# Decoding float64 weights in three instructions instead of four: the sign bit through ScalarE's leaky unit

## The chip, the core and the metric

The kernel runs on one core of a Trainium2 chip. A core has five engines that run at the same time, each with its own queue of instructions in a fixed order: TensorE (PE, matrix products, with PEld for its weight loads), VectorE (DVE), ScalarE (ACT), GpSimd (POOL) and SyncE (SP, which here only issues DMAs). An engine waits on semaphores for what another has to deliver, and whatever stands behind a waiting instruction on the same queue waits too. The metric is the device time of one execution in microseconds, less is better.

## What is computed

The reference chains three blocks. Arrays are numpy's.

```python
# attention over clusters: B, H, S, D = 2, 8, 768, 64
mask = q_assign[:, :, :, None] == k_assign[:, :, None, :]
scores = np.where(mask, scale * q @ k.T, -1e9)
attn = softmax(scores)
x = (attn @ v) reordered to (1536, 512)
# first block: w1, w2 (512, 1024), w3 (1024, 1024), w_out (1024, 512)
x = ((x @ w1) * (x @ w2)) @ w3 @ w_out
# second block: w_in (512, 2048), w_out (2048, 512)
h = x @ w_in
out = (np.maximum(h, 0) + np.log1p(np.exp(-np.abs(h)))) @ w_out
```

The weight matrices come as float64. [...]

## The kernel before

**Stages.** Three stages follow one another. Attention (to about 375 us of the profiled execution) goes through 96 slots, six per head; in slot s PE computes the scores of slot s for the row minima (`mx_pe`, line 625), then those of slot s-9 again for the exponential (`st_pe`, 652), then the product with v of slot s-10 (`av_pe`, 668). The head pairs that come later are prepared in between: norms, transposes, the cluster assignment, and DMAs on SP's queue (`t_dma` 325, `m_dma` 443) that put the pieces of q and k in place. Beside all that the product w3 @ w_out is formed in 24 pieces of 128 x 512 (`w_step`, 579), so that the first block needs only `W3O` later. The first block (375 to 569 us) multiplies 512 tokens at a time by 8 chunks of w1 and w2 and by `W3O`; the second block (569 us to the end) by 16 chunks of w_in and w_out, with the softplus between the two on ACT, DVE and POOL (`sp1`, `sp2`, `sp3`, 1082 to 1107).

**The order of work.** Within attention the order on every engine is that of the code (`tc.manual_schedule`, line 911, up to the opening of the first block); from there on a planner orders the instructions by priority, its own costs and buffer limits, and `feed.take` is held behind the last evaluation (`tc.issue_after`).

**A decode.** A piece is a DMA of 512 KB into a raw tile of 128 x 1024 words (`load_w`, 74), low and high word of each number alternating. Four instructions of 128 x 512 follow:

1. ACT multiplies the high words, read as float32, by 2^-112 (line 63). This lowers the exponent so that, three bits further left, it is float32's.
2. DVE shifts the low words right by 29 (lines 104, 489, 764).
3. DVE takes the two top bits of the scaled high word, the sign among them, and puts them into the low word (108, 493, 768).
4. DVE shifts the high word left by three, which drops the sign bit, and ors the low word in (113, 498, 773).

Then ACT rounds to the PE's format (`act_copy(hi, d)`) and POOL subtracts for the remainder (`pool_sub`, line 66). 72 pieces are decoded: 24 in `w_step`, 5 through `Feed.part` in attention's last slots, and 43 through `decode` (16 + 16 + 11), 34 of them in the first block and 9 in the second.

**Where the steps stand in the slots.** `WT` (569) gives each of the 24 pieces its steps by slot: in the piece's slot 0 A (step 1, ACT) and b (step 2), in slot 1 c (step 3), in slot 2 d (step 4), after which the next raw piece is loaded (`w_load`, 504, a DMA on SP's queue, line 81, that waits until d has read the raw tile). A new piece begins every two and a half slots. From slot 76 (`WSLOT`, lines 1000 to 1008) five more pieces go through `feed.part`, one step per slot and four slots per piece; the first two are split and stored at once (`feed.take`, slots 79 and 83), which also puts the load of a next piece on SP's queue. That load waits until POOL has finished `wl`, the remainder, since POOL reads the raw tile. The softmax's denominators travel on the same queue: `av_ev` (687) writes a row out, `r_ev` (689) reads it back as r, lets DVE invert it (699, 702), and sends it round again (704, 708).

Of the kernel before, what the change touches and what calls it, by code (L numbers as in the profile page):

```python
# [8 lines left out]
F32 = mybir.dt.float32  # L9
F32R = mybir.dt.float32r  # L10
BF16 = mybir.dt.bfloat16
I32 = mybir.dt.int32
AF = mybir.ActivationFunctionType
ALU = mybir.AluOpType
# [13 lines left out]
def fused_kernel(ctx: ExitStack, tc, q, k, v, centroids, w1, w2, w3, wo, w_in, w_o2, out):  # L28
# [6 lines left out]
    nc = tc.nc  # L35
# [23 lines left out]
    def act_copy(o, i, scale=None):  # L59
        if scale is None:  # L60
            nc.scalar.activation(o, i, AF.Copy)  # L61
        else:
            nc.scalar.activation(o, i, AF.Copy, scale=scale)

    def pool_sub(o, i, hi):
        nc.gpsimd.tensor_tensor(out=o, in0=i, in1=hi, op=ALU.subtract)  # L66

# [16 lines left out]
    def decode(pieces):  # L84

        wide, outs = [], []  # L90
        for t, o in pieces:
            if t.dtype == F32:
                if o is not None:
                    nc.vector.tensor_copy(o, t)
                outs.append(t if o is None else o)
            else:
                tv = t.rearrange("p (n t) -> p n t", t=2)
                lo, hi = tv[:, :, 0], tv[:, :, 1]
                hf = hi.bitcast(F32)
                act_copy(hf, hf, scale=2.0 ** -112)  # L100
                wide.append((lo, hi, hi if o is None else o.bitcast(I32)))
                outs.append(hf if o is None else o)
        for lo, _, _ in wide:
            nc.vector.tensor_scalar(
                out=lo, in0=lo, scalar1=29, scalar2=None, op0=ALU.logical_shift_right
            )
        for lo, hi, _ in wide:
            nc.vector.scalar_tensor_tensor(
                out=lo, in0=hi, scalar=-0x40000000, in1=lo,
                op0=ALU.bitwise_and, op1=ALU.bitwise_or,  # L110
            )
        for lo, hi, o in wide:
            nc.vector.scalar_tensor_tensor(
                out=o, in0=hi, scalar=3, in1=lo,
                op0=ALU.logical_shift_left, op1=ALU.bitwise_or,
            )
        return outs

    identF = cpool.tile([P, P], F32, name="identF")
# [351 lines left out]
    def w_scale(n):  # L471
        t = W3["r", n]
        if t.dtype != F32:
            hf = t.rearrange("p (n t) -> p n t", t=2)[:, :, 1].bitcast(F32)
            act_copy(hf, hf, scale=2.0 ** -112)

    def w_bits(n, step):

        t = W3["r", n]
        if step == 2:  # L480
            d = W3["d", n] = w3p.tile([P, 512], F32, tag="d", name=f"w3d{n}")
        if t.dtype == F32:
            if step == 2:
                nc.vector.tensor_copy(d, t)
        else:
            tv = t.rearrange("p (n t) -> p n t", t=2)
            lo, hi = tv[:, :, 0], tv[:, :, 1]
            if step == 0:
                nc.vector.tensor_scalar(
                    out=lo, in0=lo, scalar1=29, scalar2=None, op0=ALU.logical_shift_right  # L490
                )
            elif step == 1:
                nc.vector.scalar_tensor_tensor(
                    out=lo, in0=hi, scalar=-0x40000000, in1=lo,
                    op0=ALU.bitwise_and, op1=ALU.bitwise_or,
                )
            else:
                nc.vector.scalar_tensor_tensor(
                    out=d.bitcast(I32), in0=hi, scalar=3, in1=lo,
                    op0=ALU.logical_shift_left, op1=ALU.bitwise_or,  # L500
                )
        if step == 2:
            W3.pop(("r", n))
            w_load()

# [54 lines left out]
    def w3_end(n):  # L560
# [6 lines left out]


    WT = {
        "o": {0: "Ab", 1: "c", 2: "d", 6: "s"},  # L570
        "3": {0: "Ab", 1: "c", 2: "d", 3: "T", 4: "hl", 7: "m", 8: "p", 9: "q", 10: "e"},
    }
    WF = {
        "A": w_scale, "b": lambda n: w_bits(n, 0), "c": lambda n: w_bits(n, 1),
        "d": lambda n: w_bits(n, 2), "s": wo_split, "T": w3_turn, "h": w3_hi, "l": w3_lo,
        "m": w3_acc, "p": w3_add, "q": w3_out, "e": w3_end,
    }

# [160 lines left out]
    class Feed:  # L739
# [13 lines left out]
        def part(self, i, step):  # L753

            e = self.fly[i]
            t = e[0]
            if t.dtype == F32:
                return
            tv = t.rearrange("p (n t) -> p n t", t=2)
            lo, hi = tv[:, :, 0], tv[:, :, 1]  # L760
            if step == 0:
                act_copy(hi.bitcast(F32), hi.bitcast(F32), scale=2.0 ** -112)
            elif step == 1:
                nc.vector.tensor_scalar(
                    out=lo, in0=lo, scalar1=29, scalar2=None, op0=ALU.logical_shift_right
                )
            elif step == 2:
                nc.vector.scalar_tensor_tensor(
                    out=lo, in0=hi, scalar=-0x40000000, in1=lo,
                    op0=ALU.bitwise_and, op1=ALU.bitwise_or,  # L770
                )
            else:
                nc.vector.scalar_tensor_tensor(
                    out=hi, in0=hi, scalar=3, in1=lo,
                    op0=ALU.logical_shift_left, op1=ALU.bitwise_or,
                )
                self.fly[i] = (hi.bitcast(F32), e[1])

        def take(self, n=1):
# [123 lines left out]
    }  # L903


    WALL = "AbcdsThlmpqe"
    WSLOT = 76
    W0 = 4
    wk = [W0]

    with tc.manual_schedule():
        act_dma = nc.scalar.dma_start
        load_qk(0, [0])
        centroid_load()
        load_qk(0, [1], act_dma)
        nc.scalar.preload_act_table_set("natural_log_exp_and_others")
        w_load()
        w_load()
        t1_pe(0, 0)
        t1_pe(0, 1)  # L920
        centroid_prep()
        t1_ev(0, 0)
        t1_ev(0, 1)
        t1_pe(0, 2)
        t1_pe(0, 3)
        t1_ev(0, 2)
        t1_ev(0, 3)
        centroid_turn()
        norm_sq(0, 0)
        norm_sq(0, 1)  # L930
        load_qk(1)
        t_first()
        sims_pe(0, 0)
        sims_pe(0, 1)
        sims_ev(0, 0)
        sims_ev(0, 1)
        norm_sum(0, 0)
        norm_sum(0, 1)
        simsT_pe(0)
        norm_root(0)  # L940
        for n in range(W0):
            w_step(n, WALL[:1])
        norm_rec(0, 0)
        norm_rec(0, 1)
        norm_rec(0, 2)
        t_dma(0, 1)
        t_dma(0, 0)
        assign(0, 0)
        assign(0, 1)
        back_pe(0)  # L950
        back_ev(0)
        m_dma(0, 1, act_dma)
        w_load()
        load_v(0)
        for n in range(W0):
            w_step(n, WALL[1:])
        for s in range(NSLOT + ML + AL):
            j = s - ML
            a = j - AL
            if s < NSLOT:  # L960
                mx_pe(s)
                mx_red(s)
            if s and s % QC == 0 and s <= NSLOT:
                m_row(s // QC - 1)
            weights = s >= ML
            if weights:
                w_step(wk[0], "hlpqe")
            if a > 0 and a % 3 == 0:
                av_ev(a // 3 - 1)
            for tab in (PE1, EV1):  # L970
                for f, *x in tab.get(s, ()):
                    f(1, *x)
            if s == 4:
                load_qk(2)
            if s == 8:
                load_v(1)
            steps(PE, s)
            steps(EV, s)
            if 0 <= j < NSLOT:
                st_pe(j)  # L980
                st_exp(j)
            if weights:
                w_step(wk[0], "Abcds")
            if 0 <= a:
                av_pe(a)
            if weights:
                w_step(wk[0], "Tm")
                wk[0] += 1

            for g in range(NH):  # L990
                r = s - (ML + AL + QC * g + QC - 1)
                if r in (2, 4, 6):
                    r_ev(g, r // 2 - 1)
                if r == 8:
                    x_norm(2 * g)
                    x_norm(2 * g + 1)
            if wk[0] == NWSTEP:
                feed.load(3)

            if wk[0] > NWSTEP and s >= WSLOT:  # L1000
                i, k = divmod(s - WSLOT, 4)
                if i < 2:
                    feed.part(0, k)
                    if k == 3:
                        feed.take(1)
                        taken += 1
                elif i < 5:
                    feed.part(i - 2, k)
# [202 lines left out]
```

## Time and profile before

| | |
|---|---|
| runs of the kernel | 849.31, 851.35 and 854.03 us, median 851.35 |
| span of the profiled execution, first to last instruction | 846.2 us; the page lists no time of its own for that execution, the median run is 5.15 us longer than the span |
| PE busy | 798.1 us, 94% of the span |
| DVE busy | 497.7 us, 59% |
| ACT busy | 396.5 us, 47% |
| POOL busy | 245.8 us, 29% |

The profile is one execution. Busy time is an average over stages with different limits, and PE's busy time is modelled from pipelined products, so the table says which engine to look at and not what a change is worth. What a change is worth is read from the places where PE stands idle, from what released it there, and from what stood ahead of that on its own queue.

### The profile page before, as it was taken

The page shows a single profiled execution, that of the slowest core. Times are in us where ns is not written, and L with a number is a line of the kernel's source. Part 1 is how long each engine was busy: PE and PEld are TensorE (multiplying, and loading weights), DVE is VectorE, ACT ScalarE, POOL GpSimd, SP SyncE. Part 2 cuts the span into 40 slices and gives each one's busy share as a digit, 9 for nine tenths or more (in the row PEclk, how much of TensorE's full clock was granted, in tenths as well). Part 3 has the DMA queues.
Part 4 walks back from the last instruction along what each step waited for, and adds up shares of the span by engine and source line. Part 5 has one row for each costly group of instructions (what it writes and reads, how often), then busy time and mean ns, then how long its engine had stood idle before and what let it go on. Part 6 is the DMA issues. An engine that isn't in the chain of part 4 may idle for free.

```text
span 846.2 us, 10075 instructions
## 1 busy us (share of the span) xinstructions
PE 798.1 (94%) x3553; PEld 635.7 (75%) x3553; DVE 497.7 (59%) x826; ACT 396.5 (47%) x683; POOL 245.8 (29%) x232
## 2 busy tenths in 40 slices
PE   3589999979999998999999999999999999999997
PEld 3467777857777775778888888887877788888886
DVE  5878565576866565528532445564998644454443
ACT  3355445455443554555433245445555644454443
POOL 4145141145132121135201122321444222222220
PEclk9789999998999999999999999999999999999999
DMA  6875755655552555035311133430210100001001
GB/s 164 201 165 160 169 141 134 149 146 138 151 120 67 138 137 124 12 93 184 107 44 50 50 99 101 149 100 1 74 50 1 50 1 1 1 2 48 1 0 51
DMA packets 77491, 75.61 MB, mean 89 GB/s; under 512 B 46336, under 2 KB 62848, under 8 KB 77440
## 3 DMA queue, kind: packets, MB, share of 16 engines
q1 hardware_dynamic: 75476, 73.84, 32.7%
q10 hardware_dynamic: 1964, 1.12, 0.5%
q8 instruction: 28, 0.46, 0.2%
q14 instruction: 23, 0.19, 0.1%
HBM read 50.41 MB, written 3.24 MB: 63 GB/s over the span
## 4 chain that ended last, share of the span: by engine, by line
PE 77%; DVE 13%; DMA 3%; SPq 2%; ACT 2%; issue 2%; POOL 1%; DVEq 0%; POOLq 0%; ACTq 0%
PE avb L674 11%; PE rb L848 8%; PE sb L848 8%; PE sb L1073 6%; PE sb L659 6%; PE rb L1073 6%; PE mb L1142 6%; PE rb L539 5%; PE mb L870 4%; PE mb L629 3%; PE rb L1142 3%; PE avb L1142 3%; PE avb L870 2%; PE rb L870 2%; DVE mn L638 2%
## 5 line engine op out<-in xcount | busy, mean ns | idle before, releaser
L674 PE MATMUL avb<-E,v 128*128 128x384 f32 x384 | 143.3, 496 | 0.4 <-ACT t L61 0.4
L638 DVE TENSOR_REDUCE mn<-mb 128x1 f32<-128x768 f32 x92 | 87.7, 953 | 90.1 <-PE mb L629 89.5
L66 POOL TENSOR_TENSOR u<-u,t 128x512 f32<-128x512 f32 x47 | 66.7, 1420 | 167.3 <-DVE u L1096 167.3
L666 ACT ACTIVATE E<-sb 128x768 f32<-128x768 f32 x96 | 77.6, 808 | 74.3 <-PE sb L659 73.4
L659 PE MATMUL sb<-q,k 128*128 128x384 f32 (+1 forms) x384 | 92.7, 364 | 4.6 <-ACT E L666 4.0
L674 PEld LDWEIGHTS avb<-E,v 128*128 128x128 f32 x384 | 72.6, 194 | 28.8 <-ACT t L61 2.1
L629 PE MATMUL mb<-k,q 128*128 128x384 f32 x184 | 65.6, 438 | 11.6 <-DVE mn L638 9.1
L659 PEld LDWEIGHTS sb<-q,k 128*128 128x128 f32 (+1 forms) x384 | 67.8, 196 | 10.1 <-ACT E L666 6.8
L1073 PE MATMUL sb<-ys,wh_i 128*128 128x512 f32 x192 | 64.2, 395 | 3.5 <-ACT t L1084 2.2
L1073 PE MATMUL rb<-ys,wh_i 128*128 128x512 f32 x192 | 63.4, 392 | 0.0
L848 PE MATMUL rb<-xs,wh 128*128 128x512 f32 x192 | 61.7, 392 | 0.0
L848 PE MATMUL sb<-xs,wh 128*128 128x512 f32 x192 | 61.6, 392 | 0.0
L1086 DVE TENSOR_SCALAR u<-t 128x512 f32<-128x512 f32 x48 | 21.1, 440 | 68.1 <-ACT t L1085 68.1
L629 PEld LDWEIGHTS mb<-k,q 128*128 128x128 f32 x184 | 33.8, 196 | 30.9 <-DVE mn L638 13.2
L66 POOL TENSOR_TENSOR wl_o<-d_o,wh_o 128x512 fp32r<-128x512 f32 x16 | 21.6, 1351 | 121.3 <-ACT wh_o L61 121.3
L721 POOL TENSOR_TENSOR xT<-t,R 64x384 f32<-64x384 f32 x32 | 34.0, 1083 | 59.5 <-DMA R<-rd 59.3
L69 DVE TENSOR_TENSOR gl<-u,gh 128x512 fp32r<-128x512 f32 x48 | 39.6, 825 | 18.6 <-ACT gh L61 17.8
L1095 ACT ACTIVATE u<-u 128x512 f32<-128x512 f32 x48 | 30.4, 633 | 35.7 <-DVE t L1092 35.6
L1073 PEld LDWEIGHTS sb<-ys,wh_i 128*128 128x128 f32 x192 | 35.9, 188 | 13.6 <-ACT t L1084 3.3
L1073 PEld LDWEIGHTS rb<-ys,wh_i 128*128 128x128 f32 x192 | 36.1, 188 | 8.0
L848 PEld LDWEIGHTS rb<-xs,wh 128*128 128x128 f32 x192 | 36.1, 188 | 7.9
L848 PEld LDWEIGHTS sb<-xs,wh 128*128 128x128 f32 x192 | 36.1, 188 | 7.8
(208 smaller groups left out, 1787.1 us busy)
## 6 DMA issues: line engine op xcount, KB each, us to landing
w3r<-in_moe_w_dram SPq DMA_DIRECT2D x16, 512.0 KB
w12r<-in_moe_w_dram SPq DMA_DIRECT2D x16, 512.0 KB
wir<-in_moe_w_in_dram SPq DMA_DIRECT2D x16, 512.0 KB
wor<-in_moe_w_out_dram SPq DMA_DIRECT2D x16, 512.0 KB
q<-H SPq DMA_DIRECT2D x15, 384.0 KB
w3r<-in_moe_w_out_dram SPq DMA_DIRECT2D x8, 512.0 KB
k<-L SPq DMA_DIRECT2D x16, 192.0 KB
v<-in_v_dram SPq DMA_DIRECT2D x16, 192.0 KB
```

The lines of the kernel that those rows point to most:

```text
L66: nc.gpsimd.tensor_tensor(out=o, in0=i, in1=hi, op=ALU.subtract)
L69: return nc.vector.tensor_tensor(out=o, in0=i, in1=hi, op=ALU.subtract)
L539: nc.tensor.matmul(m, a[:, ks], bb, start=(mc == 0 and x == 0), stop=(mc == NK - 1 and x == 2))
L629: nc.tensor.matmul(bank[:, hf, :HALF], QT[g][:, 0, c * P : (c + 1) * P], KT[g][:, 0, hf * HALF : (hf + 1) * HALF], start=True, stop=True,)
L638: nc.vector.tensor_reduce(out=MN[g][:, c : c + 1], in_=mx_bank(s)[:, :, :HALF], op=ALU.min, axis=AX.XY)
L659: nc.tensor.matmul(sbank[:, i, :HALF], KT[g][: P - 31 * n, n, ks], QT[g][: P - 31 * n, n, qs], start=(n == 0), stop=(n == 1),)
L666: nc.scalar.activation(E[j], sbank[:, :, :HALF], AF.Exp, scale=-1.0)
L674: nc.tensor.matmul(avbank[:, :HALF], V[g][:, 2 * kp + i, :], e[:, i, :], start=(kp == 0 and i == 0), stop=(kp == 2 and i == 1),)
L848: nc.tensor.matmul(bk[:, :BLK], a[:, sl], bb, start=(n == 0), stop=(n == 3 * CC - 1))
L870: nc.tensor.matmul(ybank[e][:, :BLK], a[:, es], bb, start=(fc == 0 and n == 0), stop=(fc == NFC - 1 and n == 2),)
L1073: nc.tensor.matmul(hbank[(bl * NF2 + fc) % 4][:, :BLK], a[:, sl], bb, start=(n == 0), stop=(n == 3 * CC - 1))
L1142: nc.tensor.matmul(ob, a[:, sl], bb, start=(fc == 0 and n == 0), stop=(fc == NF2 - 1 and n == 2),)
```

## The change

The sign no longer needs step 3. Step 1 becomes an activation of the leaky kind, `Prelu`, with the same scale 2^-112 and slope `alpha` 2^32 for negative numbers. A negative number comes out 2^32 times as large, that is with 32 more in its exponent field, which sets the bit that the shift by three moves to the sign's place. Step 3 is gone at all four places. In `WT` step b moves from the piece's slot 0 to its slot 1, where c was; d stays in slot 2. In the slots from 76 on a piece takes three slots, not four: the two takes fall in slots 78 and 81, and the five pieces end in slot 90, not 95.

```diff
+    def narrow(hf):
+        nc.scalar.activation(hf, hf, AF.Prelu, scale=2.0 ** -112, alpha=2.0 ** 32)
+
+    def join(o, hi, lo):
+        nc.vector.scalar_tensor_tensor(
+            out=o, in0=hi, scalar=3, in1=lo,
+            op0=ALU.logical_shift_left, op1=ALU.bitwise_or,
+        )
...
-                act_copy(hf, hf, scale=2.0 ** -112)
+                narrow(hf)
...
-        for lo, hi, _ in wide:
-            nc.vector.scalar_tensor_tensor(
-                out=lo, in0=hi, scalar=-0x40000000, in1=lo,
-                op0=ALU.bitwise_and, op1=ALU.bitwise_or,
-            )
         for lo, hi, o in wide:
-            nc.vector.scalar_tensor_tensor(
-                out=o, in0=hi, scalar=3, in1=lo,
-                op0=ALU.logical_shift_left, op1=ALU.bitwise_or,
-            )
+            join(o, hi, lo)
...
-        "o": {0: "Ab", 1: "c", 2: "d", 6: "s"},
-        "3": {0: "Ab", 1: "c", 2: "d", 3: "T", 4: "hl", 7: "m", 8: "p", 9: "q", 10: "e"},
+        "o": {0: "A", 1: "b", 2: "d", 6: "s"},
+        "3": {0: "A", 1: "b", 2: "d", 3: "T", 4: "hl", 7: "m", 8: "p", 9: "q", 10: "e"},
...
-            elif step == 2:
-                nc.vector.scalar_tensor_tensor(
-                    out=lo, in0=hi, scalar=-0x40000000, in1=lo,
-                    op0=ALU.bitwise_and, op1=ALU.bitwise_or,
-                )
             else:
-                nc.vector.scalar_tensor_tensor(
-                    out=hi, in0=hi, scalar=3, in1=lo,
-                    op0=ALU.logical_shift_left, op1=ALU.bitwise_or,
-                )
+                join(hi, hi, lo)
...
-                i, k = divmod(s - WSLOT, 4)
+                i, k = divmod(s - WSLOT, 3)
                 if i < 2:
                     feed.part(0, k)
-                    if k == 3:
+                    if k == 2:
                         feed.take(1)
```

`w_bits` and `w_scale` change in the same way: step c is left out and A calls `narrow`.

## Rows read from the trace of the kernel before

**Rows 1.** Two stretches: PE, PEld, DVE, ACT, POOL busy (count); PEclk; DMA share; GB/s.

```profile
375.00:569.00 194.00, 194.00 (x852) 159.88 (x852) 101.97 (x169) 84.80 (x150) 51.14 (x40) 1.00 0.32 104
569.00:661.00 92.00, 88.51 (x381) 70.69 (x380) 71.48 (x98) 49.79 (x90) 34.12 (x24) 1.00 0.09 29
```

**Rows 2.** Groups on DVE, shapes apart: busy us, mean ns, then idle before and its releaser.

```profile
L493 DVE SCALAR_TENSOR_TENSOR w3r<-w3r 128x512 int32<-128x512 int32 x24 | 18.7, 781 | 0.2
...
L108 DVE SCALAR_TENSOR_TENSOR wor<-wor 128x512 int32<-128x512 int32 x16 | 15.9, 992 | 0.2
```

**Rows 3.** Waits of PE between 57 and 375 us: us in total, times, longest us.

```profile
PE mb L629 <- DVE mn L638: 6.0, 5, 3.3
PE sb L659 <- ACT E L666: 4.0, 3, 2.8
```

**Rows 4.** Timeline of DVE, 164 to 196 us: start, us, line, operation.

```profile
171.56 0.88 DVE L493 SCALAR_TENSOR_TENSOR w3r<-w3r 128x512 int32<-128x512 int32 x1
...
174.75 1.69 DVE L489 TENSOR_SCALAR w3r<-w3r 128x512 int32<-128x512 int32 x1
```

**Rows 5.** Timeline of SP's queue, 296 to 345 us.

```profile
310.69 0.35 SPq L704 DMA_DIRECT2D rd<-r  x1
313.40 0.38 SPq L81 DMA_DIRECT2D w12r<-in_moe_w_dram  x1
...
325.32 0.34 SPq L694 DMA_DIRECT2D r<-sd  x1
```

**Rows 6.** Timeline of GpSimd, 296 to 345 us.

```profile
312.07 1.30 POOL L66 TENSOR_TENSOR wl<-w12r,wh 128x512 fp32r<-128x512 f32 x1 [6.05 <-PE mb L629]
...
327.66 1.28 POOL L66 TENSOR_TENSOR wl<-w12r,wh 128x512 fp32r<-128x512 f32 x1
```

**Rows 7.** Timeline of DVE, 298 to 345 us.

```profile
310.58 0.65 DVE L773 SCALAR_TENSOR_TENSOR w12r<-w12r 128x512 int32<-128x512 int32 x1
...
326.98 2.71 DVE L699 TENSOR_SCALAR r<-r 128x6 f32<-128x6 f32 x1 [2.52 <-DMA r<-sd]
```

**Rows 8.** Timeline of PE, 298 to 345 us: the first product of three following slots.

```profile
322.66 0.81 PE L629 MATMUL mb<-k,q 128*128 128x384 f32 x2
...
325.00 0.81 PE L629 MATMUL mb<-k,q 128*128 128x384 f32 x2
...
335.50 1.12 PE L629 MATMUL mb<-k,q 128*128 128x384 f32 x2
```

**Rows 9.** Timeline of DVE, 590 to 662 us: one piece and the next one's first step.

```profile
601.85 0.41 DVE L104 TENSOR_SCALAR wir<-wir 128x512 int32<-128x512 int32 x1
602.30 1.67 DVE L108 SCALAR_TENSOR_TENSOR wir<-wir 128x512 int32<-128x512 int32 x1
604.00 0.69 DVE L113 SCALAR_TENSOR_TENSOR d_i<-wir 128x512 int32<-128x512 int32 x1
...
607.99 0.41 DVE L104 TENSOR_SCALAR wor<-wor 128x512 int32<-128x512 int32 x1
```

**Rows 10.** Timeline of GpSimd, 594 to 630 us.

```profile
602.07 1.35 POOL L66 TENSOR_TENSOR u<-u,t 128x512 f32<-128x512 f32 x1 [1.29 <-DVE u L1096]
```

**Rows 11.** Waits of PE between 600 and 661 us.

```profile
PE sb L1073 <- ACT t L1084: 2.2, 2, 1.4
PE sb L1073 <- DVE ys L69: 1.2, 1, 1.2
```

**Rows 12.** Groups on ACT, 57 to 375 us: busy us, mean ns, idle before.

```profile
L666 ACT ACTIVATE E<-sb 128x768 f32<-128x768 f32 x94 | 76.0, 808 | 73.7 <-PE sb L659 72.9
L61 ACT ACTIVATE t<-avb 128x384 f32<-128x384 f32 x31 | 15.2, 490 | 7.2 <-PE avb L674 7.2
L63 ACT ACTIVATE w3r<-w3r 128x512 f32<-128x512 f32 x21 | 14.2, 675 | 0.0
L318 ACT ACTIVATE H<-rb,qkcol 128x384 fp32r<-128x384 f32 x20 | 11.7, 583 | 30.5 <-PE rb L307 20.7 <-DMA R<-rd 4.1 <-DMA k<-H 3.8
```

**Rows 13.** The table load of line 916, the only one of the program.

```profile
L916 ACT ACT_TABLE_LOAD  x1: 1283/1283/1283, 2.4 to 2.4; - x1
```

More of the change, by code (lines that the diff above doesn't have):

```diff
@@ L474, in w_scale @@
             hf = t.rearrange("p (n t) -> p n t", t=2)[:, :, 1].bitcast(F32)
-            act_copy(hf, hf, scale=2.0 ** -112)
+            narrow(hf)
     def w_bits(n, step):
         t = W3["r", n]
-        if step == 2:
+        if step:
             d = W3["d", n] = w3p.tile([P, 512], F32, tag="d", name=f"w3d{n}")
         if t.dtype == F32:
-            if step == 2:
+            if step:
                 nc.vector.tensor_copy(d, t)
@@ L491, in w_bits @@
                 )
-            elif step == 1:
-                nc.vector.scalar_tensor_tensor(
-                    out=lo, in0=hi, scalar=-0x40000000, in1=lo,
-                    op0=ALU.bitwise_and, op1=ALU.bitwise_or,
-                )
-            else:
-                nc.vector.scalar_tensor_tensor(
-                    out=d.bitcast(I32), in0=hi, scalar=3, in1=lo,
-                    op0=ALU.logical_shift_left, op1=ALU.bitwise_or,
-                )
-        if step == 2:
+            else:
+                join(d.bitcast(I32), hi, lo)
+        if step:
             W3.pop(("r", n))
@@ L569, in fused_kernel @@
     WT = {
-        "o": {0: "Ab", 1: "c", 2: "d", 6: "s"},
-        "3": {0: "Ab", 1: "c", 2: "d", 3: "T", 4: "hl", 7: "m", 8: "p", 9: "q", 10: "e"},
+        "o": {0: "A", 1: "b", 2: "d", 6: "s"},
+        "3": {0: "A", 1: "b", 2: "d", 3: "T", 4: "hl", 7: "m", 8: "p", 9: "q", 10: "e"},
     }
     WF = {
-        "A": w_scale, "b": lambda n: w_bits(n, 0), "c": lambda n: w_bits(n, 1),
-        "d": lambda n: w_bits(n, 2), "s": wo_split, "T": w3_turn, "h": w3_hi, "l": w3_lo,
+        "A": w_scale, "b": lambda n: w_bits(n, 0), "d": lambda n: w_bits(n, 1),
+        "s": wo_split, "T": w3_turn, "h": w3_hi, "l": w3_lo,
         "m": w3_acc, "p": w3_add, "q": w3_out, "e": w3_end,
@@ L761, in part @@
             if step == 0:
-                act_copy(hi.bitcast(F32), hi.bitcast(F32), scale=2.0 ** -112)
+                narrow(hi.bitcast(F32))
             elif step == 1:
@@ L766, in part @@
                 )
-            elif step == 2:
[L768 to L771, printed above, removed]
-            else:
-                nc.vector.scalar_tensor_tensor(
-                    out=hi, in0=hi, scalar=3, in1=lo,
-                    op0=ALU.logical_shift_left, op1=ALU.bitwise_or,
-                )
+            else:
+                join(hi, hi, lo)
                 self.fly[i] = (hi.bitcast(F32), e[1])
@@ L903, in fused_kernel @@
     }
-    WALL = "AbcdsThlmpqe"
+    WALL = "AbdsThlmpqe"
     WSLOT = 76
@@ L982, in fused_kernel @@
             if weights:
-                w_step(wk[0], "Abcds")
+                w_step(wk[0], "Abds")
             if 0 <= a:
```

## The prediction

> **What bounds the kernel now.** I read the busy times by stretch first, then PE's waits inside each stage, then the timelines of the engines at those waits. In the first block PE has no free microsecond: 194.00 busy of 194, while DVE has 102 [rows 1]. Whatever DVE saves there comes to nothing. In the second block's opening, 569 to 661 us, PE is busy for 88.5 of 92 [rows 1]; its waits from 600 us on are 2.2 us for ACT's evaluation of the last product and 1.2 us for a split on DVE [rows 11], and DVE works there without a pause. In attention PE waits five times for the row minimum on DVE, 6.0 us, 3.3 of them at once, and three times for ACT's exponential, 4.0 us [rows 3]. So a shorter decode can be worth something at a handful of places, and the sum has to be made at those, not from DVE's total.
>
> **What is taken away.** 72 instructions of step 3. Undisturbed one takes about 0.69 us; their means are 781 ns in the pieces of w3 and 992 ns in those of the second matrix [rows 2], so 24 by 0.78 and 48 by between 0.69 and 0.99, 52 to 66 us of DVE's work, go. Most of it lies beside PE: attention and the first block hold 63 of the 72.
>
> *Attention, the 24 pieces.* Slot by slot the new table only lightens DVE: slot 0 loses b, slot 1 has b in place of c, slot 2 keeps d. Nothing moves to a later slot that another engine reads, and the raw tile is freed in the same slot, so SP's queue sees its loads no later. Four of the five waits for DVE together are 6.0 - 3.3 = 2.7 us [rows 3]. At two of them, around 171 to 177 us, DVE runs without a gap and carries c with 0.88 us and, in the next piece, b with 1.69 us, stretched by POOL's work beside it [rows 4]. Both stand ahead of the row minimum that PE waits for. The first becomes a b, the second goes. At the other two, around 72 to 78 us, the queue looks alike. I take 2.2 of the 2.7 us; bounds 0 (the stretched wait passes to the next instruction) and 2.7. The three waits for the exponential hang on DMAs of the next pair of heads, issued back to back on SP; they move earlier together with PE, so I take nothing, with 4.0 us as the upper bound.
>
> *Attention, the takes.* This is the largest term. In slot 79 the load of a new piece stands on SP's queue behind the issue at 310.69 (which ends at 311.04) and goes out at 313.40, because POOL's `wl` runs until 313.37 [rows 5, 6]; `wl` waits for the fourth step, which ends at 311.23 [rows 7]. SP stands still for 2.36 us, and its backlog behind that carries the row sums: the read of r is issued only at 325.32 [rows 5]. DVE meets r in its fixed order, waits 2.52 us and then needs 2.71 us for six columns, beside POOL's work, among it the second take's `wl` of 1.28 us [rows 6, 7]. The row minimum of the next slot stands behind it, and PE behind that. Undisturbed a slot takes 325.00 - 322.66 = 2.34 us; the next two take 335.50 - 325.00 = 10.50 us, so 5.8 us are lost [rows 8]. With three slots per piece the first take falls in slot 78 and lacks a step, so its `wl` is done before SP comes to the pair's DMAs; the second falls in slot 81, ahead of the slot-83 work that now stands in front of it on POOL. Moved along are, for each take, ACT's rounding, POOL's subtraction and one DMA of 512 KB. The first DMA is now ahead of a row sum's write (slot 79) and an issue of its inverse on SP; the second is ahead of one write (slot 82) and the read of r. Each costs the queue its issue of 0.38 us if `wl` is done. I take 2.3 us from SP's standstill and 1.2 us from the second `wl`, 3.5 us; bounds 0 and 5.8. What is late next there is r itself, still about 0.7 us plus part of a slot at a lowered clock.
>
> *Second block, nine pieces.* From b to the next piece's b DVE needs 607.99 - 601.85 = 6.14 us, in which step 3 takes 1.67 us and d 0.69 [rows 9]. Step 3 is long because POOL's subtraction runs from 602.07 to 603.42 [rows 10] and DVE's instruction with two tiles in SBUF ends only after it. Without step 3, d stands in that place and will take its 1.67 us. The saving per piece is then not 1.67 but 0.69, and the period 5.45 us. PE's own period is 24 products of 194.00 / 852 = 0.228 us each [rows 1], 5.46 us, so DVE just stops being the bound. Of the 2.2 + 1.2 us of waits [rows 11] I take 3.0, bounds 0 and 3.4. The loads' landing, for which ACT waits in front of that evaluation, is late next.
>
> **What is added.** `Prelu` isn't in the trace. Its nearest row is the copy with a scale that it replaces, 675 ns [rows 12]. If slope or bias came from a column in SBUF it would cost more: the copy with such a column takes 583 ns against 490 without, both 128 x 384 from PSUM [rows 12], so 93 ns each. A gain is excluded by the same shape and operands. Bounds are 0 and 72 x 0.093 = 6.7 us of ACT, which is half idle; I put 0.2 us of it on the path. In the trace no function costs a change of tables: the one load is at the start and takes 1.283 us [rows 13], though exponentials and copies alternate on ACT [rows 12]. The Trainium skill ("ScalarE: Activation LUTs", Table sets: the hidden batching unit) says that tables come in sets, that the cheap functions it lists as fillers of every set are relu, copy, identity and abs, and that a function outside the set needs a load. Prelu isn't in that list. The page (What ACT_TABLE_LOAD costs) puts a switch at about 2.66 us, twice this trace's 1.283; by its price two switches for each of attention's 29 pieces would be an estimated 154 us of ACT.
>
> **The sum.** 2.2 + 3.5 + 3.0 - 0.2 = 8.5 us. The profiled span is 846.2 us and the median run 851.35, 5.15 more; I leave that difference as it is. 851.35 - 8.5 = 842.9, forecast 843.
>
> **The rivals.** *The waits pass on.* At all three places DVE's instruction is stretched by POOL, or a DMA ends the wait. If the next instruction is stretched instead, and the waits of attention close on SP's DMAs rather than on DVE, the gain shrinks to about 2 us, 849. For it speaks that b took 1.69 us at 174.75 beside POOL, so the place and not the operation sets the price [rows 4]; against it that SP's standstill of 2.36 us has one plain cause that the change moves [rows 5, 6].
>
> *SP is blocked at a new place.* The first take's load now stands in front of the write of a row sum and the issue of its inverse. If its `wl` comes late (ACT has an exponential in front of the rounding), the r chain is held at slot 79 as the pair's DMAs were before. Then the 3.5 us are not won, and up to 2.4 us more are spent: 851.35 - 2.2 - 3.0 + 0.2 + 2.4 = 848.8. Against it: POOL had stood idle for 6.05 us when `wl` began [rows 6].
>
> *Prelu is not in the loaded tables* (the case on the slower side). Each of attention's 29 pieces then needs a load for Prelu and one for the exponential behind it, 2 x 1.283 = 2.57 us [rows 13] on ACT's queue right ahead of `E`. On the average E waits 73.7 / 94 = 0.78 us for PE [rows 12]; that covers so much, and 1.8 us reach PE: 29 x 1.8 = 52 us, 843 + 52 = 895. It decides from the fifth such piece on, where 1.8 us each have eaten the 8.5. For it speaks the page's list, by which this comes out; against it that copy, square, abs, exponential and logarithm all work from the one load.
>
> **How the numbers follow.** Half a per cent of 851.35 is 4.3 us, about what a measurement of this kernel can tell from no change; faster means under 847.1, slower over 855.6. The forecast gets 0.68, the waits passing on 0.17, the blocked SP 0.09, the tables 0.04, and 0.02 is left for a new wait of which I see no sign. Low end: all upper bounds, 2.7 + 4.0 + 5.8 + 3.4 = 15.9, gives 835.5, so 835. High end: no gain and a fair part of ACT's bound, 853; the tables' case stays out. Faster takes the forecast and a little of the first rival, 0.70; same the rest of the two rivals that end near 849, 0.24; slower the tables and what is left, 0.06.
>
> **What would show it.** Right: DVE's period in the second block's feeding stretch about 5.5 us and PE's waits there near zero; join taking over 1.6 us in some pieces, where POOL subtracts; SP's load of the first take issued without a pause and the two slots after it under 7 us; the row for ACT's narrow within 0.1 us of 675 ns; one table load in all. Wrong: PE's total for the row minimum unchanged at about 6 us, SP standing still before the write of a row sum, a second table load, or a first block that is no longer 194 us.

## The result, and the profile after

The changed kernel takes 841.57 us in the median (839.48 to 842.76, four runs), the kernel before 851.97 us beside it (849.31 to 854.03, four runs): a ratio of 0.9893, 95% interval 0.9855 to 0.9932. The forecast of 843.0 is 1.4 us off and the range holds it. Measured again beside the experiments below, the kernel before had medians of 848.21, 849.70 and 849.25 us (20, 13 and 19 runs), and the change 842.84 beside the first of these, a ratio of 0.9925 (0.9897 to 0.9953). The start of the sum, 851.35 from three runs, was thus some 2 us high, and the gain is nearer to 6 than to 10 us. The 5.15 us between that median and the profiled span, which the prediction left as they are, were a sign of it: in all other runs the time is 1.7 to 1.9 us above the span of the same run (842.76 against 840.9 in the profile of the change), so the profile of before belongs to a run of about 848 us.

The page's busy times of the changed kernel, and the two stretches of [rows 1] again:

```profile
PE 796.8 (95%) x3553; PEld 635.5 (76%) x3553; DVE 450.6 (54%) x754; ACT 396.5 (47%) x683; POOL 240.7 (29%) x232
```

```profile
375.00:569.00 194.00, 194.00 (x853) 160.05 (x852) 75.70 (x132) 84.12 (x149) 46.14 (x36) 1.00 0.30 97
569.00:661.00 92.00, 88.42 (x382) 70.97 (x382) 71.33 (x93) 50.14 (x92) 33.80 (x25) 1.00 0.09 29
```

DVE lost 47.1 us of work in all, a little under the 52 to 66 of the forecast. The first line of the two stretches is the stage where that is worth nothing: PE is busy for 194.00 of 194, and DVE has some 25 us less to do (both stages lie 5 us earlier here; from 370 to 564 us PE has 194.00 again and DVE 77.30, from 564 to 656 us PE has 88.42). The second line is the surprise. PE is busy for 88.42 of 92, where it had 88.51: the second block's opening, for which I had put in 3.0 us, has not moved.

The waits of PE, first from 57 to 375 us, to be held against [rows 3], then from 570 to 661 us, against [rows 11]:

```profile
PE sb L653 <- ACT E L660: 4.5, 3, 3.1
PE mb L623 <- DMA k<-sg: 1.9, 1, 1.9
PE mb L623 <- DVE mn L632: 1.8, 4, 1.0
```

```profile
PE sb L1059 <- ACT t L1070: 2.9, 2, 2.1
PE sb L1059 <- DVE ys L79: 0.7, 1, 0.7
```

The row minimum went from 6.0 to 1.8 us. The three waits for the exponential stayed, as the forecast took them. New in the list is a DMA, `k<-sg`, the cluster bits of the first later pair: it was late before too, by 0.6 us, and by 1.9 here. In the second block there are 3.6 us where there were 3.4, most of it for ACT as before.

To see where each part fell I read the distance between the first products of two slots in PE's timeline, in every run. This table is worked out from those timelines (us). Its slots, and those of the stretches in the expectations, are numbered one below the code's `s` (by the code the product at 325.00 in [rows 8] opens slot 86); the slots named for the takes and the steps are the code's. The last line is the second block from its first product with w_in to the last one that goes to `sb`; those to `rb` go on for 11 us more.

| stretch | before | after | what it holds |
|---|---|---|---|
| slots 10 to 11 | 3.71 | 5.07 | the wait for `k<-sg` |
| slots 11 to 12 | 2.26 | 3.45 | behind it |
| slots 13 to 18 | 16.12 | 15.51 | two of the waits of the 24 pieces |
| slots 41 to 43 | 7.38 | 5.73 | the two waits at [rows 4] |
| slots 85 to 87 | 10.50 | 5.95 | the takes, [rows 8] |
| second block | 250.1 | 249.8 | |

### The profile page after: what moved, and what is told of

Same layout as the page of the kernel before. It is cut to its first block, busy times and chain, and to the rows that moved or that the text cites. A ratio compares the mean times of both kernels' runs of the same rounds, so it can differ in the third digit from the quotient of the medians.

```text
span 840.9 us, 10003 instructions
## 1 busy us (share of the span) xinstructions
PE 796.8 (95%) x3553; PEld 635.5 (76%) x3553; DVE 450.6 (54%) x754; ACT 396.5 (47%) x683; POOL 240.7 (29%) x232
## 4 chain that ended last, share of the span: by engine, by line
PE 77%; DVE 13%; DMA 3%; ACT 3%; SPq 2%; issue 2%; POOL 1%; DVEq 0%; ACTq 0%; POOLq 0%
PE avb L668 11%; PE rb L834 8%; PE sb L834 8%; PE sb L653 6%; PE sb L1059 6%; PE mb L1128 6%; PE rb L1059 5%; PE rb L533 5%; PE mb L856 4%; PE mb L623 3%; PE rb L1128 3%; PE avb L1128 3%; DVE mn L632 2%; PE avb L856 2%; PE rb L856 2%
## 5 line engine op out<-in xcount | busy, mean ns | idle before, releaser
L1072 DVE TENSOR_SCALAR u<-t 128x512 f32<-128x512 f32 x48 | 25.5, 531 | 71.3 <-ACT t L1071 71.3
L79 DVE TENSOR_TENSOR gl<-u,gh 128x512 fp32r<-128x512 f32 x48 | 37.8, 788 | 15.7 <-ACT gh L61 15.2
```

Of the source, the lines that this page charges most:

```text
L79: return nc.vector.tensor_tensor(out=o, in0=i, in1=hi, op=ALU.subtract)
```

## Experiments

Three questions were open. Which part of the change shortens slots 85 to 87: the missing step or the takes' new place, and which take? Why did the second block gain nothing? And is the wait for `k<-sg` part of the change?

**Both kernels again.** Nothing is edited; they give the spread of the stretches.

> The changed kernel once more, unaltered. Its first profile has a span of 840.9 us, 5.3 below that of before, while the runs differ by 10.4. Theory: the first profile caught PE waiting 1.93 us (0.57 before) for the cluster bits of the second pair of heads at 58 us, with 2.6 us lost there to slot 16, by the chance of one DMA's landing and not by the change; then this profile shows the wait under 1 us, and the stage's slots 16 and later 2 to 3 us earlier than in the first profile. Rival: the step table's shift makes that transfer late; then the wait is near 1.9 us again. Time by both 840 to 843 us.

> The kernel before once more, unaltered, for a second profile. By the theory that attention's stalls are fixed by the order on the queues, the two slots after slot 84 take 10 to 11 us again, slots 41 to 43 take 7.4 us, and the second block's products of the first kind span 250 us; only the wait at 58 us may differ, between 0.5 and 3 us. By the rival that such stalls fall by chance, one of the first two is shorter by 2 us or more.

The change took 842.84 us (six runs; 848.21 beside it), the kernel before 844.86 us in one run. Slots 13 to 18 and 41 to 43 repeat within 0.02 us: 15.52 and 5.72 with the change, 16.11 and 7.37 without. Slots 85 to 87 give 6.19 and 10.33. Slots 10 to 11 do not repeat: 5.74 and 4.50, after 5.07 and 3.71. Here the theory on record failed: the wait for `k<-sg` is 2.6 us in the repeat of the change, not under 1, and 1.4 in that of the kernel before. Part of the 2.6 us that the first profile of the change has lost by slot 16 is scatter, since slots 11 to 12 took 3.45 us there and 2.23 in the repeat. Whether the change lengthens the wait itself stays open: in the three profiles whose attention decodes in four steps it is 0.6 to 1.8 us, in the eight with three steps (the last experiment, which moves a load there, left out) 0.8 to 3.4. Slots 43 to 48, where PE waits longest for the exponential, scatter as widely, from 17.40 to 20.44 us over the twelve profiles, with no order by kernel.

**The takes' place, two ways.** First the change with four slots per piece again, the third one empty, so that the takes fall in slots 79 and 83:

```diff
-                i, k = divmod(s - WSLOT, 3)
-                if i < 2:
+                i, k = divmod(s - WSLOT, 4)
+                k = (0, 1, None, 2)[k]
+                if k is None:
+                    pass
+                elif i < 2:
```

> The changed kernel with the takes of attention's last slots back in slots 79 and 83 (four slots per piece, the third left empty, join where step 4 was); the decode itself stays at three instructions. If the 4.85 us that the changed profile won between slots 85 and 88 come from where the takes stand on SP's and GpSimd's queues, they are lost again: SP's load of the first take goes out about 2 us after the issue in front of it, the two slots take about 10 us, and the time is 4 to 5 us above the changed kernel's, 845 to 847. If they come from the missing third step, the two slots take 6 us and the time stays within 1 us of it, 841 to 843.

846.51 us, a ratio of 0.9978 (0.9959 to 0.9997): most of the gain is gone. Slots 85 to 87 take 10.93 us, as long as before, though step 3 is missing in all pieces; slots 13 to 18 and 41 to 43 keep their gain (15.52 and 5.72).

Then the kernel before, with its four steps, but three slots per piece: steps 3 and 4 share the third slot, and the takes fall in 78 and 81.

```diff
-                i, k = divmod(s - WSLOT, 4)
+                i, k = divmod(s - WSLOT, 3)
+                ks = (2, 3) if k == 2 else (k,)
...
```

> The kernel before, all four steps kept, with the takes of attention's last slots in slots 78 and 81 (step 3 and step 4 of those five pieces in one slot). The first theory, that the place of the takes decides: 4 to 5 us faster than before, 847 from 852, and the two slots after slot 84 take about 6 us in place of 10.5. The rival, that the missing step decides: within 1 us of before, 851 to 853.

843.74 us, 0.9951 (0.9924 to 0.9978). Slots 85 to 87 take 4.91 us, with the step in place, and slots 41 to 43 are back at 7.37. So this part of the gain belongs to the place of the takes and not to the shorter decode.

Side by side with the same 20 runs of the kernel before (848.21 us), the shorter decode alone is thus worth 1.7 us, the takes' place alone 4.5 and both together 5.4. Most of the gain comes from the place, which a decode of four steps can have too. With the place moved, the shorter decode adds 0.9 us (843.74 to 842.84), though slots 13 to 18 and 41 to 43 give 2.3: slots 85 to 87 are longer with it, 5.95 and 6.19 for 4.91.

**One take at a time.** The forecast gave 2.3 us to the first take, for SP's standstill, and 1.2 to the second, for its `wl`. Each was put back alone.

```diff
-                if i < 2:
+                if s == 78:
+                    pass
+                elif i < 2:
+                    if s == 79:
+                        feed.part(0, 2)
+                        feed.take(1)
+                        taken += 1
                     feed.part(0, k)
-                    if k == 2:
+                    if s == 81:
```

> The changed kernel with the first take alone put back one slot, from 78 to 79; the second stays in slot 81, and the two pieces before it share the steps so. It asks which of the two takes costs slots 85 to 87. If SP's standstill behind the first take's load is the cause (the prediction's 2.3 us of 3.5), the two slots take 8 us or more again, against 5.95 in the changed kernel and 10.5 in the one before, and the run loses 2 to 4 us to the changed kernel. If the cause is POOL's second subtraction beside the scaling of the row sums on DVE, the scaling stays at 0.2 us, the two slots at 6 to 6.5 us, and the run within 1 us of the changed kernel.

```diff
-                i, k = divmod(s - WSLOT, 3)
-                if i < 2:
+                i, k = divmod(s - WSLOT - 2 * (s > 80), 3)
+                if s in (81, 82):
+                    pass
+                elif i < 2:
```

> The changed kernel with the second take alone put back, from slot 81 to 83, the pieces behind it two slots later; the first stays in slot 78. If POOL's second subtraction beside the scaling of the row sums is the cause, that scaling takes about 2.7 us again and the two slots 85 and 86 together 10 to 11 us; the run loses 3 to 5 us to the changed kernel. If SP's standstill behind the first take is the cause, the two slots stay under 7.5 us and the run loses 1 to 2 us at most.

They took 845.76 us (0.9949, 0.9925 to 0.9973) and 845.71 us (0.9950, 0.9927 to 0.9973); by the ratios each loses 2 us to the changed kernel. The two slots took 7.74 and 9.13 us, between the two theories both times: neither holds alone. With both takes moved they take 5.95, with none 10.93. The first take's place is then worth 7.74 - 5.95 = 1.8 us, or 10.93 - 9.13 = 1.8; the second's 9.13 - 5.95 = 3.2, or 10.93 - 7.74 = 3.2. The two add up, as far as single profiles tell: over the six profiles with the shorter decode and both takes moved the stretch lies between 5.91 and 6.49 us, so each share holds to about half a microsecond.

How, the timelines tell. SP's queue in the changed kernel; the row sum is written out at 322.09 (`sd<-t`) and read back as r at 325.52:

```profile
308.28 0.76 SPq L643 DMA_DIRECT2D q<-mr  x1
310.51 0.38 SPq L91 DMA_DIRECT2D w12r<-in_moe_w_dram  x1
310.99 0.31 SPq L681 DMA_DIRECT2D sd<-t  x1
...
321.46 0.53 SPq L91 DMA_DIRECT2D w12r<-in_moe_w_dram  x1
322.09 0.31 SPq L681 DMA_DIRECT2D sd<-t  x1
325.52 0.34 SPq L688 DMA_DIRECT2D r<-sd  x1
```

SP still stands for 1.47 us before the first load (308.28 + 0.76 to 310.51), where it stood for 2.36 [rows 5]. What is gained is that the write at 322.09 leaves earlier: 2.67 us before the first product of slot 85 (324.76 below), against 0.98 with the first take late. But the load of the second take now stands right in front of that write, which then needs 3.43 us until the read can go, not 2.18 as with the second take late. The rows of that write and that load, first from the queue with the first take late, then with the second late:

```profile
325.33 0.55 SPq L91 DMA_DIRECT2D w12r<-in_moe_w_dram  x1
325.97 0.31 SPq L681 DMA_DIRECT2D sd<-t  x1
329.51 0.35 SPq L688 DMA_DIRECT2D r<-sd  x1
```

```profile
317.88 0.38 SPq L681 DMA_DIRECT2D sd<-t  x1
320.06 0.34 SPq L688 DMA_DIRECT2D r<-sd  x1
323.68 0.38 SPq L91 DMA_DIRECT2D w12r<-in_moe_w_dram  x1
324.15 0.78 SPq L643 DMA_DIRECT2D q<-mr  x1
```

So in the changed kernel the read is no earlier by the slot than before: 0.76 us behind the first product of slot 85, where it was 0.32 [rows 5, 8]. The rest is line 693 (699 before) on DVE, which adds 1e-9 to r; the expectations call it the scaling. In the changed kernel's timelines of DVE, GpSimd and PE:

```profile
327.26 0.17 DVE L693 TENSOR_SCALAR r<-r 128x6 f32<-128x6 f32 x1 [3.05 <-DMA r<-sd]
```

```profile
316.16 1.30 POOL L76 TENSOR_TENSOR wl<-w12r,wh 128x512 fp32r<-128x512 f32 x1 [2.76 <-ACT wh L61]
```

```profile
324.76 0.80 PE L623 MATMUL mb<-k,q 128*128 128x384 f32 x2
...
328.55 0.62 PE L623 MATMUL mb<-k,q 128*128 128x384 f32 x2 [0.99 <-DVE mn L632]
...
330.71 0.81 PE L623 MATMUL mb<-k,q 128*128 128x384 f32 x2
```

Six columns take 0.17 us, where they took 2.71 [rows 7], because this `wl` was done ten microseconds before. With the first take late, where this `wl` is done early too, it is 0.17 again. With the second take late, DVE and GpSimd show the stretch once more:

```profile
321.70 1.97 DVE L693 TENSOR_SCALAR r<-r 128x6 f32<-128x6 f32 x1 [1.07 <-DMA r<-sd]
```

```profile
322.36 1.29 POOL L76 TENSOR_TENSOR wl<-w12r,wh 128x512 fp32r<-128x512 f32 x1
```

DVE's instruction ends at 323.67 and `wl` at 323.65. SP's standstill comes in a second time there: the load that waits for this `wl` goes out at 323.68, `q<-mr` only behind it at 324.15, and PE waits another 1.2 us for `q<-mr` (0.6 in the kernel before). And PE's granted clock fell behind these pauses, to 0.50, the lower level of 1.2 GHz, from 328 to 330 us with the second take late and from 334 to 336 in the kernel before; in the changed kernel and with the first take late it stayed at 1.00 from 328 to 338. Those are the parts of the 3.2 us, which were not measured one by one.

**The second block.** The timelines of DVE and ACT in the changed kernel, one piece:

```profile
602.97 1.66 DVE L70 SCALAR_TENSOR_TENSOR d_o<-wor 128x512 int32<-128x512 int32 x1
605.85 1.10 DVE L1072 TENSOR_SCALAR u<-t 128x512 f32<-128x512 f32 x1 [1.22 <-ACT t L1071]
...
609.44 1.66 DVE L70 SCALAR_TENSOR_TENSOR d_i<-wir 128x512 int32<-128x512 int32 x1
...
615.91 1.67 DVE L70 SCALAR_TENSOR_TENSOR d_o<-wor 128x512 int32<-128x512 int32 x1
...
621.32 1.67 DVE L70 SCALAR_TENSOR_TENSOR d_i<-wir 128x512 int32<-128x512 int32 x1
```

```profile
602.56 0.58 ACT L1070 ACTIVATE t<-rb 128x512 f32<-128x512 f32 x1
604.66 0.63 ACT L61 ACTIVATE wh_o<-d_o 128x512 fp32r<-128x512 f32 x1 [1.53 <-DVE d_o L70]
605.20 0.61 ACT L1071 ACTIVATE t<-t 128x512 f32<-128x512 f32 x1
```

The join took the stretched 1.66 us in step 3's place, as forecast. But the period is 609.44 - 602.97 = 6.47 us, longer than the 6.14 of [rows 9], because DVE now stands idle for 1.22 us in front of `u`. `u` needs the exponential (line 1071), and ACT runs the rounding `wh_o` ahead of it; the rounding waits 1.53 us for the join. The planner, which orders this stage, had put the exponential first in the kernel before. Now, in three of the four passes seen between 596 and 622 us, the rounding comes first; in the fourth the exponential does, and the next join follows after 621.32 - 615.91 = 5.41 us. From the join at 596.48 the four together take 24.84 us, 6.21 each, against 6.14 in the kernel before. So the change alters an order that its diff does not touch. The test holds the rounding behind the exponential of the same pass:

```diff
-        def take(self, n=1):
+        def take(self, n=1, after=None):
...
             for (hi, lo), d in zip(tiles, ds):
-                act_copy(hi, d)
+                if after is None:
+                    act_copy(hi, d)
+                else:
+                    with tc.issue_after(after.ins):
+                        act_copy(hi, d)
                 pool_sub(lo, d, f32(hi))
...
-        nc.scalar.activation(t, t, AF.Exp, scale=-1.0)
+        ex[0] = nc.scalar.activation(t, t, AF.Exp, scale=-1.0)
...
-                feed.take()
+                feed.take(after=ex[0])
```

> The changed kernel, with ACT's rounding of a decoded piece in the second block queued behind the exponential of the same pass. In the changed profile the planner put the rounding, which waits for the join, in front of that exponential, and DVE stood still 1.22 us a piece for the exponential; the period from one join to the next stayed 6.47 us. If that order ate the second block's expected gain, the period falls to about 5.5 us, PE's waits between 560 and 661 us from 3.6 us to under 1, and the time by 2.5 to 3.5 us below the changed kernel's, 838 to 839.5. If DVE's work with GpSimd beside it is the bound whatever ACT's order, the period stays above 6 us and the time within 1 us of the changed kernel's.

837.48 us (837.00 to 838.42), 0.9875 (0.9848 to 0.9903), beside the same runs of the kernel before as the change's 0.9925; by the medians that is 5.4 us below the change, more than the first theory's 2.5 to 3.5. The second block takes 245.4 us. ACT and DVE, of the same stretch, and its windows:

```profile
596.22 0.63 ACT L1075 ACTIVATE t<-t 128x512 f32<-128x512 f32 x1
596.88 0.64 ACT L61 ACTIVATE wh_i<-d_i 128x512 fp32r<-128x512 f32 x1
```

```profile
595.18 1.67 DVE L70 SCALAR_TENSOR_TENSOR d_i<-wir 128x512 int32<-128x512 int32 x1
596.88 0.43 DVE L1076 TENSOR_SCALAR u<-t 128x512 f32<-128x512 f32 x1
...
617.50 1.66 DVE L70 SCALAR_TENSOR_TENSOR d_i<-wir 128x512 int32<-128x512 int32 x1
```

```profile
560.00:650.00 90.00, 90.00 (x393) 73.25 (x392) 68.78 (x94) 53.01 (x95) 35.61 (x25) 1.00 0.09 30
```

Four pieces take 617.50 - 595.18 = 22.3 us, 5.58 each, and PE has no gap left (87.15 of 90 in the changed kernel). Is it the order alone, then? Step 3 was put back into the 43 pieces of `decode`, once in the changed kernel and once with the exponential first:

```diff
+        for lo, hi, _ in wide:
+            nc.vector.scalar_tensor_tensor(
+                out=lo, in0=hi, scalar=-0x40000000, in1=lo,
+                op0=ALU.bitwise_and, op1=ALU.bitwise_or,
+            )
         for lo, hi, o in wide:
             join(o, hi, lo)
```

> The changed kernel with step 3 put back into `decode` alone, that is in all 43 pieces after attention (the sign bit is then set twice, with the same value); the 29 pieces of attention keep three instructions. If the missing step is worth nothing in the second block while the planner puts the rounding in front of the exponential, the second block's products of the first kind span 250 us as in before and in the changed kernel, and the time is the changed kernel's within 1 us, 842 to 844. If the second block does owe the missing step part of the gain and only the profile hid it, the time is 3 us above, 845 to 847.

> Step 3 put back into `decode` alone, and the rounding queued behind the exponential as in the run that did that to the changed kernel (837.5 us, second block's products of the first kind in 245.4 us). If order and missing step are needed together, since four instructions keep DVE at 6.14 us a piece, the span is back at 249 to 250 us and the time near 842. If the order alone makes the gain, it stays at 245 to 246 us and 838.

The second block takes 251.0 and 250.0 us. With the step alone gone it takes 249.8 and 251.5 (the change and its repeat), with the order alone set 250.0, with both 245.4, and 245.4 once more in the next experiment. Either part alone brings nothing and the two together 4.7 us. By the runs the changed kernel with step 3 back in 43 of 72 pieces takes 841.64 us, 0.9908 (0.9878 to 0.9938), no more than without it; with the exponential first it takes 841.28, 0.9907 (0.9870 to 0.9943).

**The load behind the cluster bits.** On top of the exponential first, the load of a raw piece that SP issues in slot 9 goes behind the four DMAs of cluster bits of the same pair.

```diff
-            w_load()
+            if held is None:
+                w_load()
+            else:
+                held.append(n)
...
+    held = None
...
+            if s == ML:
+                held = []
+            if s == ML + 1:
+                nh, held = len(held), None
+                for _ in range(nh):
+                    w_load()
```

> The changed kernel with the rounding behind the exponential, and one DMA moved: the load of a raw piece that stands on SP's queue at 50 us in front of the four cluster-bit DMAs of the second pair goes behind them. In six profiles PE waits 0.6 to 2.6 us for the last of these at 58 us, in two of them the slots after it run slower by some 2 us more. If that wait comes from the 512 KB in flight and the place on the queue, the DMA lands 1 to 3 us earlier, the wait is 0, and the time 1 to 3 us below 837.5. If it comes from the data's own readiness, nothing moves: 836.5 to 838.5.

834.81 us (832.99 to 835.76), 0.9822 (0.9791 to 0.9852): the best kernel of the study, faster than both, and as the first theory has it 1 to 3 us below 837.5. SP's queue in the changed kernel and in this one:

```profile
50.42 0.33 SPq L91 DMA_DIRECT2D w3r<-in_moe_w_dram  x1
50.86 0.58 SPq L448 DMA_DIRECT2D q<-sg  x1
...
52.75 0.60 SPq L448 DMA_DIRECT2D k<-sg  x1
```

```profile
50.57 0.59 SPq L448 DMA_DIRECT2D q<-sg  x1
...
52.48 0.59 SPq L448 DMA_DIRECT2D k<-sg  x1
53.17 0.53 SPq L91 DMA_DIRECT2D w3r<-in_moe_w_dram  x1
```

And PE there, in the same order:

```profile
58.03 0.58 PE L623 MATMUL mb<-k,q 128*128 128x384 f32 x2 [1.93 <-DMA k<-sg]
61.48 1.26 PE L623 MATMUL mb<-k,q 128*128 128x384 f32 x2
```

```profile
55.67 0.59 PE L626 MATMUL mb<-k,q 128*128 128x384 f32 x2 [0.57 <-DMA k<-sg]
```

The bits are issued 0.3 us earlier, and PE goes on 2.4 us earlier. The wait is 0.57 us, not the 0 of the first theory. From the issue of the last of the four DMAs to PE's product it is 3.19 us here (52.48 to 55.67) and 5.28 in the changed kernel (52.75 to 58.03); in the other ten profiles with the load in front it is 4.2 to 5.4. So the place of the load is worth about 1.0 to 2.2 us here.

## Why the prediction was right, and where not

The size and the sign came out, the sum less so: 2.2 + 3.5 + 3.0 - 0.2 stands against 2.3 + 4.6 + 0.3 - 0, read from the first two profiles.

*The 24 pieces*: right. Slots 13 to 18 gave 0.61 and slots 41 to 43 1.65 us, 2.26 for 2.2, and both came in every run that had the shorter decode, wherever the takes stood. b, which slid into c's place, was itself stretched a little, to 0.97 us from c's 0.88 [rows 4]; the b of 1.69 us is gone from the path:

```profile
173.02 0.97 DVE L491 TENSOR_SCALAR w3r<-w3r 128x512 int32<-128x512 int32 x1
```


*The takes*: the cause was right and the term mis-sized, 3.5 for 4.6 (10.50 to 5.95; 10.33 to 6.19, 4.1, in the repeats; 1.8 by the first take and 3.2 by the second in the runs with one take put back). The shares were the wrong way round. The step that failed was "I take 2.3 us from SP's standstill and 1.2 us from the second `wl`". That the first take's `wl` "is done before SP comes to the pair's DMAs" did not hold: SP was free at 309.04 and stood until 310.51. So its standstill did not vanish, it shrank and moved, and a 512 KB load came to stand ahead of the write that r is read from. The second `wl` cost more than its own length: DVE's addition, the load that blocks `q<-mr`, and then the clock. "What is late next there is r itself" held: 0.99 us are left.

*The second block*: wrong, 0.3 for 3.0. The stretched join was right, "the period 5.45 us", "so DVE just stops being the bound", was not. That step summed DVE's own instructions and left out that DVE also waits for ACT, whose order a planner writes anew for every version. With the old order the term would have been 4.7, above the bound of 3.4 too. That bound counted PE's idle time; by [rows 1] 381 products at 0.228 us fill only 86.8 of the 92 us, so 5.2 were open, and with the exponential first 393 products fill 89.5 of 90.

*Prelu*: right at zero. ACT's group in attention and the only table load:

```profile
L67 ACT ACTIVATE w3r<-w3r 128x512 f32<-128x512 f32 x21 | 14.0, 668 | 0.0
```

```profile
L902 ACT ACT_TABLE_LOAD x1 | 1.3, 1283 | 2.4 <-issue 2.4
```

668 ns stand against 675 [rows 12], and there is one load in the program, as before. The rival on the slower side is out. The Trainium skill ("ScalarE: Activation LUTs", Table sets: the hidden batching unit) lists the fillers of every set without Prelu; by these rows Prelu needed no load of its own beside exponentials and logarithms.

*The other rivals.* "The waits pass on" holds at one of its three places: in the second block DVE's work became a wait for ACT. In attention it holds in small: of the 2.3 us of the 24 pieces about 1 comes back in slots 85 to 87. There PE comes to slot 85 1.44 us earlier than with four steps and the same takes (324.76 for 326.20), but the write of the row sum leaves only 0.60 earlier (322.09 for 322.69). That is one profile on the side of the four steps. "SP is blocked at a new place" is seen in small, 1.47 us at 309. The write right behind it left later than before, at 310.99 for 309.56; the next one, which slots 85 to 87 wait for, left earlier, at 322.09 for 323.13.

*Of what was to be seen*: the period of 5.5 us and the waits near zero did not come, nor did the load without a pause, and of the signs of being wrong SP's standstill before the write of a row sum did; the join above 1.6 us, the two slots under 7 us, the narrow and the one table load did. PE's first block stayed at its length.

The right total owes something to chance as well: the terms that were too large and too small nearly cancel, and the forecast started from a median of three runs, 851.35, where more runs gave 848 to 850. From the 848 us of the profiled execution the same sum would have given 839.5.

## What to carry to other kernels

Where an instruction is taken out, read again the order in which a planner then puts the others: here a rounding came to stand in front of an exponential on which more depends; why the planner put it there these runs don't show. Place a large transfer, or an elementwise pass on GpSimd, by what stands behind it on its queue and beside it on VectorE; here the place of two takes was by itself worth 4.5 us, and 72 instructions of VectorE less, by themselves, 1.7. And test each part alone: in the second block order and shorter decode were worth nothing alone and 4.7 us together.

## What the runs showed of the hardware

**VectorE beside GpSimd.** On the pieces of w_out the price belonged to the place and not to the operation. The join's group there now has the mean that step 3 had, 990 ns for 992 [rows 2], while the same instruction on the pieces of w1 and w2 that go through `decode` takes 682. Over the program, the five groups of step 3 made 59.9 us of DVE's work in the kernel before, and DVE's busy time fell by 47.1: the other 12.8 came back as longer instructions elsewhere. Two groups of the changed kernel on DVE:

```profile
L70 DVE SCALAR_TENSOR_TENSOR d_o<-wor 128x512 int32<-128x512 int32 x16 | 15.8, 990 | 0.2
...
L70 DVE SCALAR_TENSOR_TENSOR d<-w12r 128x512 int32<-128x512 int32 x9 | 5.9, 682 | 0.2
```

Beside the join that starts at 602.97 GpSimd ran this subtraction:

```profile
602.74 1.34 POOL L76 TENSOR_TENSOR u<-u,t 128x512 f32<-128x512 f32 x1 [2.55 <-DVE u L1082]
```

It ended at 604.08, and the join at 604.63, 0.55 us behind it. The Trainium skill ("SBUF — State Buffer", Summary: rules for kernel authors) says that of a VectorE instruction with two inputs in SBUF and a GpSimd instruction that reads SBUF, the one that issues second is blocked until the first ends. The join agrees. The addition on six columns, which has one input, waited longer than for one instruction: in the kernel before, its 2.71 us end at 329.69 [rows 7], and `wl`, in front of which it started, had ended at 328.94 [rows 6]; two fills on GpSimd followed without a gap.

**The granted clock.** In the changed kernel PE was busy for 0.10 of the 2 us from 56 to 58, waiting for `k<-sg`. The clock was then 0.76 from 58 to 60 us, 0.50 (1.2 GHz) from 60 to 62, 0.89 from 62 to 64, and 1.00 after that. The slot behind took 3.45 us, not 2.26. In the repeat of the change PE was busy for 0.14 of those 2 us and waited 2.6 us, longer still, and the clock stayed at 1.00 with a slot of 2.23. So a pause of this kind cost another 1.2 us in one execution and nothing in another; what decides it these runs don't show, and it is one source of the scatter between runs of one kernel.
